# Turning the scaled rows of six chunks by DMA transpose instead of TensorE

## The chip, the cores and the metric

The kernel runs on one core of one Trainium2 chip. The metric is the device time of one execution in microseconds (us). A profiled execution gives a span, from the first to the last instruction, and a time of its own that is a little longer.

## The reference

Polynomial-sketch attention for 4 batches x 4 heads x 1088 positions with head size 32, followed by a two-layer network with squared ReLU over all 4352 tokens:

```python
def phi(x):
    a = np.einsum('rd,bhsd->bhsr', S1, x)          # r = 8
    b = np.einsum('rd,bhsd->bhsr', S2, x)
    return np.einsum('bhsi,bhsj->bhsij', a, b).reshape(*x.shape[:-1], 64)

q_p, k_p = (phi(q), phi(k))
kv = np.einsum('bhsf,bhsd->bhfd', k_p, v)
z = np.sum(k_p, axis=2)
num = np.einsum('bhsf,bhfd->bhsd', q_p, kv)
den = np.einsum('bhsf,bhf->bhs', q_p, z)[..., None] + 1e-06
attn = num / den
x = attn.transpose(0, 2, 1, 3).reshape(4352, 128)  # heads side by side
h = np.maximum(x @ w_in, 0.0)                      # w_in 128 x 2048
out = h * h @ w_out                                # w_out 2048 x 128
```

## The kernel before

The tokens of a batch are cut into two chunks of 512 (`(b, g)` with `b` 0 to 3 and `g` 0 or 1) and 64 leftover rows. Chunk (0,0) is done in two halves of 256 at the start, and the leftover rows of all four batches make one chunk of 256 near the end. So there are ten chunks in the order: two halves, (0,1), (1,0), (1,1), (2,0), (2,1), (3,0), the leftover rows, (3,1).

*The network.* `first_product` (L694) makes `pg`, 128 hidden features x 512 tokens, from `xT` (the chunk's rows turned so that the 128 features lie on the partitions) and a block of `w_in`, both in 16 bits; ScalarE takes the ReLU into `gt` (L701), VectorE squares it into `g` (L702, `g2` in the source). `block` multiplies `g` by a block of `w_out` into `po` (L721; L731 for the last chunk). There are 16 such steps to a chunk. `first_product` runs up to two steps ahead of `block`, over the border to the next chunk if that one is in the list `chunks`. The results are scaled back by `beta` and stored by `store` (L667, L675).

*The attention.* It is cut into generators whose pieces are worked in between the steps of the network: `add_work` puts them in lanes, and after each step `pump(2)` lets up to two lanes advance. `yield n` in a generator asks for n steps until its next piece; `drain` runs all lanes to their end. `k_gen` makes the sums over keys (`kvbd`) of the next batch, `q_gen` the features of the queries of a chunk, and `x_gen` the numerators `nd`, the scaled rows `xs` and `xT`.

*The turning of xs.* `normalize` computes for each row the denominators, a scale per row and `beta`, and writes `xs` (VectorE, L469: 128 positions x 512, four blocks of 128 features, 16 bits). Two steps later TensorE transposes the four blocks into a PSUM tile `x_ps` (L484), and ScalarE copies it to `xT` (L487). Then `chunk_of` puts the chunk in `chunks`.

*The loads.* All loads and stores are issued on SP. The `k`, `v` and `q` of batch b+2 are loaded in the middle of the work on batch b, after the first `drain`; they are pinned: `keep_in_program_order` holds them in the place that the source gives them. `v` is brought by 32 small DMAs (L110, tile `v_turned`), which GpSimd copies into `v_main` (L359). The chunks that are not in `BY_PE` have their q, and for b > 1 their k, turned in 32 x 32 blocks by VectorE (`turned`, L241, tile `xt`).

The start, up to `by_hand.close()`, is in an order written by hand; after it a scheduler orders the instructions of each engine by its own estimates. Each engine works its queue in order.

Of the kernel before, what the change touches and what calls it, by code (L numbers as in the profile page):

```python
# [12 lines left out]
def _v(t: bass.AP, off: int, free, p0: int = 0, n: int = 128):  # L13

    p = list(t.ap)[0]
    return bass.AP(
        t.tensor, t.offset + p0 * p[0] + off, [[p[0], n]] + [list(d) for d in free]
    )
# [3 lines left out]
def kernel(  # L22
# [11 lines left out]
    nc = tc.nc  # L34
# [374 lines left out]
    def numerators(b, phT, m, T=4, tag="nd", bufs=1):  # L409
        nd = pspool.tile([128, 256 * T], F32, name="nd", tag=tag, bufs=bufs)  # L410
        for t in range(T):
            for pr in range(2):
                tiled(
                    nd, 256 * t + 2 * VW * pr, 2 * VW, phT[pr], 128 * t,
                    kvbd[b % 2][:, 2 * VW * pr : 2 * VW * pr + 2 * VW],
                    m=m,
                )
        return nd
# [4 lines left out]
        nc.gpsimd.memset(t[:], 1.0)  # L423
    made_norms = [0]

    def normalize(nd, T, xT, col):


        small = [apool.tile([128, 16], F32, name=f"small{i}", tag=f"small{i}") for i in range(4)]
        den, rden, top, rs = small  # L430
        rtop = rtops[made_norms[0] % len(rtops)]
        made_norms[0] += 1
        mm = apool.tile([128, 4], F32, tag="mm")
        mp = apool.tile([128, 4], F32, tag="mp")
        rm = apool.tile([128, 4], F32, tag="rm")
        beta = apool.tile([128, 4], F32, tag="beta", bufs=4)
        xs = apool.tile([128, 512], F16, tag="xs")
        num = _v(nd, 0, [[256, T], [VW, 4], [1, 32]])
        nc.vector.tensor_scalar(
            out=den[:, 0 : 4 * T], in0=_v(nd, D, [[256, T], [VW, 4]]),  # L440
            scalar1=1e-6, scalar2=None, op0=add,
        )
        nc.vector.reciprocal(rden[:, 0 : 4 * T], den[:, 0 : 4 * T])
        nc.vector.tensor_reduce(
            out=_v(top, 0, [[4, T], [1, 4]]), in_=num,
            axis=AX, op=amax, apply_absolute_value=True,
        )
        yield 1
        nc.vector.tensor_tensor(  # L449
            out=_v(rtop, 0, [[5, T], [1, 4]]),  # L450
            in0=_v(top, 0, [[4, T], [1, 4]]),
            in1=_v(rden, 0, [[4, T], [1, 4]]),
            op=mult,
        )
        nc.vector.tensor_reduce(  # L455
            out=mm[:, 0:T], in_=_v(rtop, 0, [[5, T], [1, 5]]),
            axis=AX, op=amax, apply_absolute_value=True,
        )
        nc.vector.reciprocal(rm[:, 0:T], mm[:, 0:T])
        nc.vector.scalar_tensor_tensor(  # L460
            out=_v(rs, 0, [[4, T], [1, 4]]),
            in0=_v(rden, 0, [[4, T], [1, 4]]),
            scalar=1024.0,
            in1=_v(rm, 0, [[1, T], [0, 4]]),
            op0=mult,
            op1=mult,
        )
        yield 1
        nc.vector.tensor_tensor(  # L469
            out=_v(xs, 0, [[128, T], [32, 4], [1, 32]]),  # L470
            in0=num,
            in1=_v(rs, 0, [[4, T], [1, 4], [0, 32]]),
            op=mult,
        )
        nc.gpsimd.tensor_scalar(  # L475
            out=mp[:, 0:T], in0=mm[:, 0:T], scalar1=1.0 / 1024.0, scalar2=None, op0=mult
        )
        nc.gpsimd.tensor_tensor(
            out=beta[:, 0:T], in0=mp[:, 0:T], in1=mp[:, 0:T], op=mult
        )  # L480
        yield 2
        x_ps = pspool.tile([128, 512], F16, tag="ms", bufs=2)
        for t in range(T):
            nc.tensor.transpose(  # L484
                x_ps[:, 128 * t : 128 * t + 128], xs[:, 128 * t : 128 * t + 128], iden16[:, :]
            )
        nc.scalar.copy(xT[:, col : col + 128 * T], x_ps[:, 0 : 128 * T])  # L487
        return beta
# [5 lines left out]
    def chunk_of(b, g, xT, beta):  # L494
        at = out.offset + (b * S + 4 * g) * E
        if (b, g) in BY_PE:
            dsts = [(bass.AP(out.tensor, at, [[NJ * E, 128], [1, 512]]), 0, 128, 0, 512)]
        else:
            dsts = [
                (  # L500
                    bass.AP(
                        out.tensor, at + j * E, [[NJ * E, 32], [32 * NJ * E, 4], [1, E]]
                    ),
                    32 * j, 32, 0, 512,
                )
                for j in range(4)
            ]
        chunks.append((xT, 4, [(beta, 4)], dsts))

    def half_gen(phT, t0, m, tag, bufs):  # L510

        nd = numerators(0, phT, m, 2, tag, bufs)
        yield 1
        xT = apool.tile([128, 256], F16, name="xT_h", tag=f"xT_h{t0}", bufs=1)
        beta = yield from normalize(nd, 2, xT, 0)
        dst = bass.AP(out.tensor, out.offset + t0 * E, [[NJ * E, 128], [1, 256]])
        chunks.append((xT, 2, [(beta, 2)], [(dst, 0, 128, 0, 256)]))
        yield 1

    def x_gen(b, g, phT, m=32):  # L520
        nd = numerators(b, phT, m)
        yield 1
        xT = apool.tile([128, 512], F16, name="xT", tag="xT", bufs=3)
        beta = yield from normalize(nd, 4, xT, 0)
        chunk_of(b, g, xT, beta)
        yield 1

    def q_gen(b, g, outer, m=32):
        eng = nc.scalar
        if (b, g) == (0, 1):  # L530
            ph = features(ab_second[0], 4, "ph_q", eng, outer)
        else:
            xt = proj_t(q_sb[b], g, 4, eng) if (b, g) in BY_PE else turned(q_sb[b], g)
            yield 1
            ph = proj(xt, 4, "ph_q", eng, outer, m=m)
        yield 3
        phT = []
        for pr in range(2):
            phT.append(feature_t(ph, 4, pr, eng))
            yield 1  # L540
        yield from x_gen(b, g, phT)
# [19 lines left out]
    def qrem_num_gen(b):  # L561
        r, u = b // 2, b % 2
        if u == 0:
            nd_rem[r] = cpool.tile([128, 4 * VW], F32, name=f"nd_rem{r}")
        nd = pspool.tile([128, 512], F32, name="nd", tag="ms", bufs=2)
        for pr in range(2):
            tiled(
                nd, 2 * VW * pr, 2 * VW, phT_rem[r][pr], 64 * u,
                kvbd[u][:, 2 * VW * pr : 2 * VW * pr + 2 * VW], 64, 64 * u,
            )  # L570
        nc.vector.tensor_copy(
            out=_v(nd_rem[r], 0, [[1, 4 * VW]], 64 * u, 64),
            in_=_v(nd, 0, [[1, 4 * VW]], 64 * u, 64),
        )
        yield 1
        if u == 1:
            beta = yield from normalize(nd_rem[r], 1, xT_rem, 128 * r)
            rem_beta.append((beta, 1))
            for w in range(2):
                dst = bass.AP(  # L580
                    out.tensor, out.offset + ((2 * r + w) * S + SM) * E, [[E, 64], [1, E]]
                )
                rem_dst.append((dst, 64 * w, 64, 128 * r, 128))
            if r == 1:
                chunks.append((xT_rem, 2, rem_beta, rem_dst))
# [292 lines left out]
```

## Time and profile before

| | |
|---|---|
| median of 3 runs | 212.81 us (212.15 to 213.9) |
| profiled execution, its own time | 213.51 us |
| its span | 211.4 us |
| granted TensorE clock | 0.999 |
| TensorE busy | 202.8 us, 96% |
| VectorE busy | 146.2 us, 69% |
| ScalarE busy | 111.8 us, 53% |
| GpSimd busy | 48.0 us, 23% |
| transposes of xs (L484) | 34, six groups of four in the chunks that are changed |
| copies to xT (L487), 128x512 | 7, 585 ns each |

Busy time is the sum over an engine's instructions; a group's row has the line, the engine, the operation, what it writes and reads, its shape and number, then busy time, the mean ns of one, and the idle time of the engine before them with what ended it. `PE` is TensorE, `PEld` its weight loads, `DVE` VectorE, `ACT` ScalarE, `POOL` GpSimd, and `SPq` SP issuing a DMA. A row of the timeline has start and duration in us, the engine, the line and the instruction; in brackets is how long the engine sat idle before it, and what released it.

### The profile page before, as it was taken

Reading aid. Unit: us, or ns where it says so; the run is one execution under the profiler, and the core shown is the slowest. Engines: PE = TensorE matmul, PEld = TensorE weight load, DVE = VectorE, ACT = ScalarE, POOL = GpSimd, SP = SyncE. Lnnn points to the kernel's source line nnn. Section 1 sums busy time; section 2 is a strip of 40 time slices with the busy share of each in tenths; the row PEclk is TensorE's granted clock in tenths of the full one; section 3 lists DMA queues with packets and bytes.
Section 4 is the critical chain, followed back from the end, with each engine's and each line's share of the span. In section 5 each row is a group of like instructions: output and inputs, shape, how many; then the busy total and the mean of one; then the engine's idle time right before and its main releaser. Section 6 shows DMA issues by size and latency. Waiting matters only on the chain.

```text
span 211.4 us, 5448 instructions
## 1 busy us (share of the span) xinstructions
PE 202.8 (96%) x2241; PEld 127.4 (60%) x2241; DVE 146.2 (69%) x281; ACT 111.8 (53%) x212; POOL 48.0 (23%) x66
## 2 busy tenths in 40 slices
PE   6988999999999999999999999999999899999993
PEld 5876878764644545545545555455445454789992
DVE  3559766936586899867777677567858777766662
ACT  2448664354556455455465553655465456555550
POOL 1003364104040683004130971022102210000000
PEclk9999999999999999999999999999999999999999
DMA  6999101422400421131000200001000100010001
GB/s 167 243 355 291 18 0 31 129 36 31 137 0 0 142 46 31 31 109 50 3 2 2 54 3 3 0 15 38 0 0 4 48 3 0 2 50 16 12 0 50
DMA packets 25736, 11.36 MB, mean 54 GB/s; under 512 B 13296, under 2 KB 25328, under 8 KB 25712
## 3 DMA queue, kind: packets, MB, share of 16 engines
q1 hardware_dynamic: 25632, 11.02, 19.9%
q8 instruction: 17, 0.28, 0.5%
q14 instruction: 7, 0.06, 0.1%
q10 hardware_dynamic: 80, 0.01, 0.0%
HBM read 8.79 MB, written 2.23 MB: 52 GB/s over the span
## 4 chain that ended last, share of the span: by engine, by line
PE 89%; DVE 6%; DMA 1%; ACT 1%; issue 1%; ACTq 0%; DVEq 0%
PE po L721 47%; PE pg L694 14%; PE po L731 7%; PE ab_ps L204 5%; PE nd L204 4%; PE kv_ps L309 3%; PE t_ps L386 3%; DVE g L702 3%; PE xt_ps L224 2%; PE o_ps L638 2%; DMA s_nat<-in_S_dram 1%; PE x_ps L484 1%; ACT gt L701 1%; DVE xs L469 1%; DVE rtop L449 1%
## 5 line engine op out<-in xcount | busy, mean ns | idle before, releaser
L702 DVE TENSOR_TENSOR g<-gt 128x512 f32<-128x512 f32 x136 | 102.3, 763 | 44.1 <-ACT gt L701 42.0
L721 PE MATMUL po<-g,w_o 128*128 128x512 f32 (+1 forms) x288 | 123.5, 525 | 1.2 <-DVE g L702 1.2
L701 ACT ACTIVATE gt<-pg 128x512 f32<-128x512 f32 x136 | 81.3, 599 | 47.7 <-PE pg L694 46.1
L721 PEld LDWEIGHTS po<-g,w_o 128*128 128x128 f32 x288 | 52.3, 191 | 26.5 <-issue 8.4
L245 POOL TENSOR_TENSOR ph<-ab 128x512 f32<-128x512 f32 (+1 forms) x27 | 32.6, 1234 | 61.5 <-ACT ab L59 61.5
L694 PE MATMUL pg<-xT,w_in 128*128 128x512 f16 x112 | 42.5, 381 | 0.0
L694 PEld LDWEIGHTS <-w_in 128*128 128x128 f16 x160 | 15.5, 99 | 20.1 <-issue 16.4
L475 POOL TENSOR_SCALAR mp<-mm 128x4 f32<-128x4 f32 (+2 forms) x11 | 5.4, 494 | 61.6 <-DVE mm L455 61.6
L731 PEld LDWEIGHTS po<-w_o,g 128*128 128x128 f32 x128 | 16.6, 192 | 0.6
L731 PE MATMUL po<-w_o,g 128*128 128x128 f32 x128 | 16.6, 275 | 0.0
L59 ACT COPY sb<-t_ps 128x512 f32<-128x512 f32 (+1 forms) x18 | 9.1, 515 | 9.9 <-PE t_ps L386 9.8
L204 PEld LDWEIGHTS ab_ps<-w_bd,xt 128*32 128x32 f32 (+1 forms) x476 | 9.6, 119 | 6.4 <-issue 3.5
L59 ACT COPY ab<-ab_ps 128x256 f32<-128x256 f32 (+1 forms) x19 | 6.3, 338 | 13.1 <-PE ab_ps L204 11.5
L204 PE MATMUL ab_ps<-w_bd,xt 128*32 128x64 f32 (+1 forms) x476 | 12.9, 230 | 0.0
L386 PEld LDWEIGHTS t_ps<-iden,ph 128*128 128x128 f32 x60 | 7.5, 141 | 6.8 <-issue 4.9
L204 PEld LDWEIGHTS nd<-kvbd,sb 128*32 128x32 f32 x480 | 8.0, 109 | 6.0 <-issue 3.6
L204 PE MATMUL nd<-kvbd,sb 128*32 128x66 f32 x480 | 9.9, 222 | 0.6 <-issue 0.6
L386 PE MATMUL t_ps<-iden,ph 128*128 128x128 f32 x60 | 9.2, 273 | 0.0
L487 ACT COPY xT<-x_ps 128x512 f16<-128x512 f16 x7 | 4.1, 585 | 9.6 <-PE x_ps L484 9.6
L59 ACT COPY xt<-xt_ps 128x512 f32<-128x512 f32 (+1 forms) x11 | 5.2, 471 | 6.4 <-PE xt_ps L224 6.3
L667 DVE TENSOR_TENSOR o_sb<-o_ps,beta 128x512 f32<-128x512 f32 (+2 forms) x10 | 5.5, 557 | 3.1 <-PE o_ps L638 2.9
L694 PE MATMUL pg<-xT_h,w_in 128*128 128x256 f16 x32 | 6.0, 273 | 0.6 <-ACT gt L701 0.5
(70 smaller groups left out, 120.9 us busy)
## 6 DMA issues: line engine op xcount, KB each, us to landing
t<-in_k_dram SPq DMA_DIRECT2D x3, 512.0 KB, 4.0
t<-in_q_dram SPq DMA_DIRECT2D x3, 512.0 KB, 4.0
out_dram<-o_sb SPq DMA_DIRECT2D x20, 64.0 KB, 1.8
w_in<-in_moe_w_in_dram SPq DMA_DIRECT2D x2, 512.0 KB, 5.0
w_o<-in_moe_w_out_dram SPq DMA_DIRECT2D x2, 512.0 KB, 7.5
v_turned<-in_v_dram SPq DMA_DIRECT2D x64, 16.0 KB, 1.7
k_sb<-in_k_dram SPq DMA_DIRECT2D x2, 256.0 KB, 3.3
q_sb<-in_q_dram SPq DMA_DIRECT2D x2, 256.0 KB, 4.9
```

What stands on the lines that cost most here:

```text
L59: return nc.scalar.copy(dst, src)
L204: nc.tensor.matmul(out_ps[p0 + c : p0 + c + m, c0 : c0 + w], lhsT[:, l0 + c : l0 + c + m], rhs,)
L245: eng.tensor_tensor(out=_v(ph, 256 * t0, [[64, 4 * w], [8, 8], [1, 8]]), in0=_v(ab, 64 * t0, [[16, 4 * w], [1, 8], [0, 8]]), in1=_v(ab, 64 ...
L309: nc.tensor.matmul(self.ps[c : c + self.m, at : at + w], _v(ph, c0 + 128 * pr + c, [[1, self.m]], p0, n), v_of(2 * pr + c // 64), start=c ...
L386: nc.tensor.transpose(t_ps[:, 128 * t : 128 * t + 128], ph[:, 256 * t + 128 * pr : 256 * t + 128 * pr + 128], iden[:, :],)
L475: nc.gpsimd.tensor_scalar(out=mp[:, 0:T], in0=mm[:, 0:T], scalar1=1.0 / 1024.0, scalar2=None, op0=mult)
L667: nc.vector.tensor_tensor(out=_v(o_sb, 128 * t0, [[128, n], [1, 128]]), in0=_v(po, 128 * t0, [[128, n], [1, 128]]), in1=_v(beta, 0, [[1, n ...
L694: nc.tensor.matmul(pg[:, nt * i : nt * i + nt], w_in[:, 128 * (c + i) : 128 * (c + i) + 128], xT[:, 0:nt],)
L701: last_relu[0] = nc.scalar.activation(gt[:, :], pg[:, :], Relu).ins
L702: nc.vector.tensor_tensor(out=g2[:, :], in0=gt[:, :], in1=gt[:, :], op=mult)
L721: last_product[0] = nc.tensor.matmul(po[0][:, 0:nt], w_o[:, 128 * c : 128 * c + 128], g2[:, nt * i : nt * i + nt], start=(c == 0), stop=(c ...
L731: nc.tensor.matmul(po[t // 2][:, 128 * (t % 2) : 128 * (t % 2) + 128], g2[:, 128 * t : 128 * t + 128], w_o[:, 128 * c : 128 * c + 128], st ...
```

## The change

The four transposes on TensorE and the copy on ScalarE are replaced by one DMA transpose, issued on SP, that reads `xs` and writes `xT`, both in SBUF. It is done for the six chunks (1,0) to (3,1); chunk (0,1), the two halves and the leftover rows keep the old way. The chunk is put in the list four steps later than the DMA is issued, for chunk (0,1) four steps later than its copy. All lines behind the change move by up to six: `pg` becomes L700, its ReLU L707, the square L708, `po` L727 and L737, the store L681, and the DMA transpose is L482.

```diff
-    def normalize(nd, T, xT, col):
+    def normalize(nd, T, xT, col, by_dma=False):
...
         nc.gpsimd.tensor_tensor(
             out=beta[:, 0:T], in0=mp[:, 0:T], in1=mp[:, 0:T], op=mult
         )
+        if by_dma:
+            nc.sync.dma_start_transpose(
+                _v(xT, col, [[128, T], [1, 128]]), xs[:, 0 : 128 * T]
+            )
+            return beta
         yield 2
         x_ps = pspool.tile([128, 512], F16, tag="ms", bufs=2)
...
-        beta = yield from normalize(nd, 4, xT, 0)
+        beta = yield from normalize(nd, 4, xT, 0, by_dma=(b, g) != (0, 1))
+        yield 4
         chunk_of(b, g, xT, beta)
```

## The prediction

> **What bounds the kernel now.** I read first the page's shares by engine and the chain that ended last, then the timeline of TensorE around one of the six removed groups, then the two queues that the change moves work onto (SP) or past (VectorE).
>
> ```profile
> span 211.4 us, 5448 instructions
> PE 202.8 (96%) x2241; PEld 127.4 (60%) x2241; DVE 146.2 (69%) x281; ACT 111.8 (53%) x212; POOL 48.0 (23%) x66
> PE 89%; DVE 6%; DMA 1%; ACT 1%; issue 1%; ACTq 0%; DVEq 0%
> L484 PE MATMUL x_ps<-iden,xs 128*128 128x128 f16 x34 | 3.7, 220 | 0.2 <-DVE xs L469 0.2
> L487 ACT COPY xT<-x_ps 128x512 f16<-128x512 f16 x7 | 4.1, 585 | 9.6 <-PE x_ps L484 9.6
> ```
>
> TensorE is busy 96% of the span and is 89% of the chain. Whatever leaves its queue is a gain; whatever it has to wait for is a loss. ScalarE, at 53%, is not the bound, so evictions taken from it bring nothing by themselves. The x_ps group holds 34 transposes: 24 belong to the six chunks of the change, the other ten to the two halves, chunk (0,1) and the leftover rows. What one group of four costs TensorE is read from the distance between neighbouring `pg` products:
>
> ```profile
> 61.22 0.38 PE L694 MATMUL pg<-xT,w_in 128*128 128x512 f16 x1
> 61.44 1.12 PE L721 MATMUL po<-g,w_o 128*128 128x512 f32 x2
> 62.40 0.39 PE L484 MATMUL x_ps<-iden,xs 128*128 128x128 f16 x4
> 62.62 0.38 PE L694 MATMUL pg<-xT,w_in 128*128 128x512 f16 x1
> 63.70 0.38 PE L694 MATMUL pg<-xT,w_in 128*128 128x512 f16 x1
> 64.77 0.38 PE L694 MATMUL pg<-xT,w_in 128*128 128x512 f16 x1
> ```
>
> With the four transposes in between, the step is 62.62 - 61.22 = 1.40 us; without, 1.07 or 1.08. One group costs 0.33 us. The product at 64.77 is the first that reads the new chunk's xT.
>
> **Part 1, the gain.** Six groups x 0.33 = 1.9 us leave TensorE's path. Six evictions x 0.585 = 3.5 us leave ScalarE; they lie beside products (the step after one, 62.62 to 63.70, is the usual 1.08), so I count 0 for them. In the built program the order of TensorE's queue is otherwise that of before, so the late addition of the chunk (the new `yield 4`) moves no product. Gain: 1.9 us, and no more than that.
>
> **Part 2, the latency L of the transposing DMA.** It may start when xs is written and must have landed before the chunk's first `pg`. The room is that product's start, less 0.33 (its queue is now shorter), less 0.1 (its weight load, which carries the wait), less the end of xs. For (1,0), xs ends at 60.06 + 0.69 = 60.75: 64.77 - 0.43 - 60.75 = 3.6 us. The same reading gives 3.6 for (2,0) (xs ends 106.71, product 110.72), 3.6 for (3,0) (152.17, 156.16), 5.6 for (2,1) (129.40, 135.46) and 12.7 for (3,1) (174.89, 187.98). What covers the transfer is four steps of 1.07 us; anything over the room stops TensorE one for one, since its queue is in order.
>
> No transpose by DMA is in this trace, so L is bounded by rows:
>
> ```profile
> q1 hardware_dynamic: 25632, 11.02, 19.9%
> out_dram<-o_last SPq DMA_DIRECT2D x2, 128.0 KB, 1.9
> v_turned<-in_v_dram SPq DMA_DIRECT2D x64, 16.0 KB, 1.7
> v_rem<-in_v_dram SPq DMA_DIRECT2D x4, 32.0 KB, 4.1
> ```
>
> From below: a plain 128 KB transfer, which is what xs holds, lands in 1.9 us. From above: a packet of the queue took 19.9% x 16 x 211.4 / 25632 = 26 ns of one engine. The built instruction gives its unit as 16 rows by 128 columns, so a unit has 16 elements for each of 128 partitions; written as separate pieces that is 4,096 of them, 4,096 x 26 ns / 16 = 6.7 us, and with the 1.7 of a small DMA 8.4. I take 4.1, the row of short pieces, near the geometric middle. Then (1,0), (2,0) and (3,0) stick out by 0.5 us each, 1.5 together; (2,1) and (3,1) are covered.
>
> The skill's pages disagree. The Trainium skill, "Advanced Engine Details and Errata", section X-Bar Transpose (TRN2), holds such transfers as fast as regular ones; L would then be near the plain row, this term 0, and the sum below -0.1 us, 212.7. "VectorE: DVE Perf Modes", section The three transpose paths, speaks against the change: 1309 ns by DMA against 390 on TensorE for one 128x128 block. Four in a row are an estimate of 5.2 us, this term 4.8, and the sum +6.1 us, 218.9. The trace's 0.33 us for four blocks already beats the page's TensorE price.
>
> **Part 3, what waits behind the transpose on SP.** SP's queue is in order. In the built program the transpose of (1,1) stands ahead of the pinned loads for batch 3 (k, 32 pieces of v, q), which before went out as soon as the store ahead of them had. Before, and the same load for batch 2, for which VectorE did wait:
>
> ```profile
> 35.82 0.38 SPq L79 DMA_DIRECT2D t<-in_k_dram  x1
> 39.89 0.71 DVE L241 STREAM_TRANSPOSE xt<-t 128x512 f32<-128x512 f32 x1 [0.23 <-DMA t<-in_k_dram]
> ...
> 70.93 0.39 SPq L79 DMA_DIRECT2D t<-in_k_dram  x1
> 71.37 18.85 SPq L110 DMA_DIRECT2D v_turned<-in_v_dram  x32
> 90.26 0.43 SPq L79 DMA_DIRECT2D t<-in_q_dram  x1
> ...
> 84.56 0.71 DVE L241 STREAM_TRANSPOSE xt<-t 128x512 f32<-128x512 f32 x1
> 85.19 0.65 DVE L469 TENSOR_TENSOR xs<-nd,small 128x512 f16<-128x512 f32 x1
> 87.16 0.71 DVE L241 STREAM_TRANSPOSE xt<-t 128x512 f32<-128x512 f32 x1
> ```
>
> The k load of batch 3 goes out at 70.93, 13.6 us before its first reader at 84.56. Now it stands behind a wait for xs of (1,1). In the built program the two turns of that k (84.56 and 87.16) come later on VectorE, behind the copies of kvbd, so xs ends 0.54 us earlier against its neighbours, and 0.33 for the group saved in (1,0): 85.84 - 0.87 = 84.97. The transpose goes out at 85.05, the k load 0.45 later (four stores took 1.78 to issue) at 85.50. With the 4.07 us of batch 2 (35.82 to 39.89) it lands at 89.57; that is the lower end. The upper: it runs in the same queue q1 behind the transpose and lands no sooner than 85.05 + 4.1 + 2.27, where 2.27 is 4.07 less the 1.8 of a small store: 91.42. Rows for either are lacking; I take the middle, 90.5.
>
> VectorE is at the first turn at about 87.9 and stops there, 2.6 us, with the squares g queued behind it. The order is turn, g, turn, g: the first g is done 0.71 + 0.69 = 1.40 after the landing, the second 2.80. Their readers, the `po` pairs at 90.22 and 91.30 of before, are now due 0.66 earlier, 89.56 and 90.64. TensorE stops for the later of landing + 1.40 - 89.56 and landing + 2.80 - 90.64, which is landing - 87.8. That is 90.5 - 87.8 = 2.7 us (1.8 at the lower end, 3.6 at the upper). The xT of (1,1) has 90.00 - 0.43 - 85.30 = 4.3 us of room and lies within this wait. The v pieces (18.85 us) and q follow until about 105; the copies of v on GpSimd (106.18) and the turn of that q (118.31) still find them, and with four stores (1.8 us) SP is free near 107, when xs of (2,0), pushed back by the stall, is just ready. I count 0 there; without the stall it would be about 1 us.
>
> **Sum.** -1.9 + 1.5 + 2.7 = +2.3 us. The profiled run took 213.51 us, span 211.4 and 2.1 around it; it becomes 215.8. The median of the three runs is 212.81, 0.7 less: 215.1, or 1.1% slower. About 1% is what a measurement of this kernel can tell from no change (the three runs lie within 0.8%).
>
> **Rivals.**
> *The transfer is hidden and the late k costs little (not slower).* One mechanism: L at or under 3.6 us, so every room covers it, and k at its lower end. -1.9 + 1.8 = -0.1: 212.7. Were k's wait absent as well, -1.9: 210.9. For it: DMA engines that are idle then (slices 12 and 13 of the span, at (1,0), and 21, at (2,0), show 0 tenths) and the 1.9 us row. Against: batch 2, where VectorE waited for k although no transpose was ahead. It decides from L = 3.6.
> *The transfer becomes the bound.* At L = 7, three chunks lose 3.4 each, (2,1) 1.4, and k, between 89.57 and 94.32, 4.1: 10.2 + 1.4 + 4.1 - 1.9 = +13.8, 226.6. At 8.4 it is +20, 233. For it: 26 ns a packet. Against: 4,096 separate pieces are only inferred from the unit's shape.
> *It does not use a fast path and moves element by element.* 65,536 elements x 26 ns / 16 = 106 us for each of six: beyond 700 us. Against: the instruction is one of its own kind, not a strided copy.
>
> **How the numbers follow.** Forecast (L 3.6 to 5.5): 0.45; hidden: 0.30; bound: 0.22; elementwise: 0.03. The likeliest gives 215.1, its own range 212.7 to 220. For 8 in 10 I leave out the upper half of the bound case, the elementwise one, and the best corner of the hidden one: 211.2 to 226. Faster by over 1% needs more than the 1.9 us there is: 0.05 for what I do not see. Within 1%: the hidden case less that, and a fifth of the forecast: 0.34. Slower: 0.61.
>
> **What would show it.** Right: no x_ps groups at six places; distances of 1.07 there; VectorE's L241 waiting 2 to 4 us for `t<-in_k_dram` near 88 us; weight loads of L700 (the line of `pg` after the change) waiting about half a microsecond for xT at (1,0), (2,0), (3,0). Wrong: a transpose issue that lands within 3.6 us or takes over 5.5; SP issuing k of batch 3 near 71 us as before; a L241 that does not wait.

## The result, and the profile after

The changed kernel takes 215.35 us (median of 22 runs, 214.03 to 217.82), the kernel before 212.83 (22 runs). The ratio is 1.0112, 95% interval 1.0093 to 1.0132: about 2.4 us slower, 2.0 to 2.8. Of the 22 runs eight show a granted TensorE clock of 1.0 and have a median of 214.77 us, the others 0.984 or 0.992 and a median of 216.0 us. The profiled execution, one of the eight, took 214.32 us, with a span of 212.6. That span is only 1.2 us above the one of before. But the first product starts at 17.72 us before and at 16.48 after, a difference of 1.24 us that arises in a stretch where no instruction was changed, so the spans are compared here step by step and not as totals.

The page of the changed kernel, in its parts: span, busy time, the large queue, the chain by engine, the group of VectorE's block turns, and the new DMA with its time from issue to landing.

```profile
span 212.6 us, 5409 instructions
PE 201.0 (95%) x2217; PEld 124.7 (59%) x2217; DVE 145.3 (68%) x281; ACT 108.9 (51%) x206; POOL 47.8 (22%) x66
q1 hardware_dynamic: 28896, 11.81, 21.1%
PE 82%; DVE 8%; DMA 3%; ACT 2%; issue 2%; ACTq 0%; SPq 0%; DVEq 0%
L241 DVE STREAM_TRANSPOSE xt<-t 128x512 f32<-128x512 f32 x9 | 6.2, 701 | 3.5 <-DMA t<-in_k_dram 3.5
xT<-xs SPq DMA_TRANSPOSE x6, 2.3
```

The group of the block turns before:

```profile
L241 DVE STREAM_TRANSPOSE xt<-t 128x512 f32<-128x512 f32 x9 | 6.2, 700 | 0.2 <-DMA t<-in_k_dram 0.2
```

TensorE has 24 matmuls fewer and is busy 1.8 us less, yet its share of the chain fell from 89% to 82%: VectorE and DMA came in. The group rows point at the reason: before the block turns of L241, VectorE now sits idle 3.5 us for the k load, where it was 0.2. The DMA transposes themselves land in 2.3 us (the median of the six), and the queue q1 moved 28896 - 25632 = 3264 packets more, 544 for each of six.

The timeline at (1,0) shows the gain and the room:

```profile
60.08 1.30 SPq L482 DMA_TRANSPOSE xT<-xs  x1
60.52 0.38 PE L700 MATMUL pg<-xT,w_in 128*128 128x512 f16 x1
60.74 1.12 PE L727 MATMUL po<-g,w_o 128*128 128x512 f32 x2
61.70 0.38 PE L700 MATMUL pg<-xT,w_in 128*128 128x512 f16 x1
62.77 0.38 PE L700 MATMUL pg<-xT,w_in 128*128 128x512 f16 x1
63.85 0.38 PE L700 MATMUL pg<-xT,w_in 128*128 128x512 f16 x1
```

The step that held the group, 1.40 us before, is now 61.70 - 60.52 = 1.18. It did not fall to 1.07, so the group cost 0.22 and not 0.33. The product at 63.85 is the first that reads the new xT, and it comes on the beat of 1.08: 60.08 + 2.3 = 62.4 is early enough.

The timeline at (1,1) shows the loss. First the products of before, then the changed kernel:

```profile
90.00 0.38 PE L694 MATMUL pg<-xT,w_in 128*128 128x512 f16 x1
91.08 0.38 PE L694 MATMUL pg<-xT,w_in 128*128 128x512 f16 x1
92.15 0.38 PE L694 MATMUL pg<-xT,w_in 128*128 128x512 f16 x1
```

```profile
83.76 0.69 DVE L469 TENSOR_TENSOR xs<-nd,small 128x512 f16<-128x512 f32 x1
84.48 1.20 SPq L482 DMA_TRANSPOSE xT<-xs  x1
85.77 0.54 SPq L79 DMA_DIRECT2D t<-in_k_dram  x1
88.89 0.38 PE L700 MATMUL pg<-xT,w_in 128*128 128x512 f16 x1
90.58 0.71 DVE L241 STREAM_TRANSPOSE xt<-t 128x512 f32<-128x512 f32 x1 [3.30 <-DMA t<-in_k_dram]
91.21 0.65 DVE L708 TENSOR_TENSOR g<-gt 128x512 f32<-128x512 f32 x1
91.92 1.12 PE L727 MATMUL po<-g,w_o 128*128 128x512 f32 x2 [2.65 <-DVE g L708]
92.88 0.38 PE L700 MATMUL pg<-xT,w_in 128*128 128x512 f16 x1
94.07 0.38 PE L700 MATMUL pg<-xT,w_in 128*128 128x512 f16 x1
```

Read the second view from the top. SP waits for xs, spends 1.20 us on issuing the transpose, and only then sends the k load of batch 3, at 85.77 instead of 70.93. VectorE waits 3.30 us for its landing, the square of L708 stands behind it, and the `po` pair behind the square. The two products at 88.89 and 92.88 are 3.99 apart, the next two 1.19; before, the same steps were 91.08 - 90.00 = 1.08 and 1.07. That is 2.91 + 0.12 = 3.03 us.

Set against each other product by product, the two profiles differ in these steps: six groups, -1.30 us together (0.20 to 0.22 each, at (1,1) net of sums over keys that became 0.14 slower); the wait for k, +3.03; and the sums over keys near 131 us, +0.13. The sum is +1.86. One more step of +0.53 lies near 42 us, ahead of anything that was changed for TensorE:

```profile
42.56 0.42 PE L204 MATMUL nd<-kvbd,sb 128*32 128x66 f32 x7 [0.56 <-issue]
41.85 0.42 PE L204 MATMUL nd<-kvbd,sb 128*32 128x66 f32 x7 [1.09 <-issue]
```

The first row is of before, the second of the changed kernel; `issue` is idle time in which the engine waited for nothing that the profile shows. This step is taken up below.

### The profile page after: what moved, and what is told of

Same layout as the page of the kernel before. It is cut to its first block, busy times and chain, and to the rows that moved or that the text cites. A ratio compares the mean times of both kernels' runs of the same rounds, so it can differ in the third digit from the quotient of the medians.

```text
span 212.6 us, 5409 instructions
## 1 busy us (share of the span) xinstructions
PE 201.0 (95%) x2217; PEld 124.7 (59%) x2217; DVE 145.3 (68%) x281; ACT 108.9 (51%) x206; POOL 47.8 (22%) x66
## 3 DMA queue, kind: packets, MB, share of 16 engines
q1 hardware_dynamic: 28896, 11.81, 21.1%
## 4 chain that ended last, share of the span: by engine, by line
PE 82%; DVE 8%; DMA 3%; ACT 2%; issue 2%; ACTq 0%; SPq 0%; DVEq 0%
PE po L727 44%; PE pg L700 13%; PE po L737 7%; PE nd L204 4%; PE ab_ps L204 4%; DVE g L708 4%; PE t_ps L386 3%; PE kv_ps L309 3%; DMA t<-in_k_dram 2%; PE xt_ps L224 2%; PE o_ps L644 2%; ACT gt L707 1%; DMA s_nat<-in_S_dram 1%; DVE xs L469 1%; DVE xt L241 1%
## 5 line engine op out<-in xcount | busy, mean ns | idle before, releaser
L708 DVE TENSOR_TENSOR g<-gt 128x512 f32<-128x512 f32 x136 | 101.6, 758 | 42.4 <-ACT gt L707 40.7
L727 PE MATMUL po<-g,w_o 128*128 128x512 f32 (+1 forms) x288 | 123.7, 526 | 3.9 <-DVE g L708 3.9
L707 ACT ACTIVATE gt<-pg 128x512 f32<-128x512 f32 x136 | 81.2, 599 | 57.2 <-PE pg L700 55.6
L727 PEld LDWEIGHTS po<-g,w_o 128*128 128x128 f32 x288 | 52.1, 191 | 31.4 <-issue 10.8
L700 PE MATMUL pg<-xT,w_in 128*128 128x512 f16 x112 | 42.5, 381 | 0.0
L700 PEld LDWEIGHTS <-w_in 128*128 128x128 f16 x160 | 15.5, 99 | 21.4 <-issue 17.6
L737 PEld LDWEIGHTS po<-w_o,g 128*128 128x128 f32 x128 | 16.6, 191 | 0.6
L737 PE MATMUL po<-w_o,g 128*128 128x128 f32 x128 | 16.6, 275 | 0.0
L204 PEld LDWEIGHTS ab_ps<-w_bd,xt 128*32 128x32 f32 (+1 forms) x476 | 8.9, 113 | 6.7 <-issue 3.5
L204 PE MATMUL ab_ps<-w_bd,xt 128*32 128x64 f32 (+1 forms) x476 | 12.2, 224 | 0.2
L241 DVE STREAM_TRANSPOSE xt<-t 128x512 f32<-128x512 f32 x9 | 6.2, 701 | 3.5 <-DMA t<-in_k_dram 3.5
L700 PE MATMUL pg<-xT_h,w_in 128*128 128x256 f16 x32 | 6.0, 274 | 0.6 <-ACT gt L707 0.5
```

Source lines behind the costliest of these rows:

```text
L204: nc.tensor.matmul(out_ps[p0 + c : p0 + c + m, c0 : c0 + w], lhsT[:, l0 + c : l0 + c + m], rhs,)
L241: nc.vector.transpose(out=xt[:, :], in_=_v(src, 128 * g, [[NJ * D, 4], [1, 128]]))
L700: nc.tensor.matmul(pg[:, nt * i : nt * i + nt], w_in[:, 128 * (c + i) : 128 * (c + i) + 128], xT[:, 0:nt],)
L707: last_relu[0] = nc.scalar.activation(gt[:, :], pg[:, :], Relu).ins
L708: nc.vector.tensor_tensor(out=g2[:, :], in0=gt[:, :], in1=gt[:, :], op=mult)
L727: last_product[0] = nc.tensor.matmul(po[0][:, 0:nt], w_o[:, 128 * c : 128 * c + 128], g2[:, nt * i : nt * i + nt], start=(c == 0), stop=(c ...
```

## The experiments

Theory A: the loss is the k load of batch 3 behind the transpose of (1,1) on SP; the transposes themselves are hidden. Theory B: each DMA transpose costs about the same, 0.4 us, by its transfer or by what it disturbs.

**Five chunks by DMA, all but (1,1).**

```diff
-        beta = yield from normalize(nd, 4, xT, 0, by_dma=(b, g) != (0, 1))
-        yield 4
+        by_dma = (b, g) not in ((0, 1), (1, 1))
+        beta = yield from normalize(nd, 4, xT, 0, by_dma=by_dma)
+        if by_dma:
+            yield 4
```

> Five chunks by DMA; (1,1) is turned on TensorE as before, so the loads of batch 3 go out near 71 us again. Theory A (the loss is the k load of batch 3 behind the transpose of (1,1)): five groups x 0.21 us saved, about 0.1 lost at the sums over keys near 131 us, no wait of VectorE for k: 0.9 us under the kernel before, ratio 0.996. Theory B (each transpose by DMA costs about the same, 2.4 us / 6): +2.0 us, ratio 1.009. In the trace by A: the L241 of k at 84 to 87 us without a wait, the matrix products of the sums over keys near 86 us at 1.30 us and near 131 us at 1.43.

Measured: ratio 0.9933, interval 0.9905 to 0.9961, 1.4 us faster than the kernel before. Theory B is out: five sixths of the transposes bring a gain. The timeline of this kernel has the second k turn without a wait, and the two sums over keys, the first with no transpose in flight, the second with that of (2,1):

```profile
85.57 0.70 DVE L241 STREAM_TRANSPOSE xt<-t 128x512 f32<-128x512 f32 x1
84.40 1.29 PE L309 MATMUL kv_ps<-v_main,ph 128*32 128x33 f32 x128
128.26 1.42 PE L309 MATMUL kv_ps<-v_main,ph 128*32 128x33 f32 x128
```

**Only (1,1) by DMA.** The same edit with `by_dma = (b, g) == (1, 1)`.

> Only (1,1) by DMA, the other five on TensorE as before. Theory A: the whole wait is kept, +3.0, less one group of 0.21: +2.8 us over the kernel before, ratio 1.013, slower than with all six. Theory B: +0.4 us, ratio 1.002. In the trace by A: one L241 that waits some 3.3 us for the k load.

Measured: 1.0166 (1.0126 to 1.0206), 3.5 us slower. One transpose of six brings more than the whole loss, which is what A says; the size is above the 2.8 expected, at the edge of the interval (2.7 to 4.4). Its timeline:

```profile
85.84 1.31 SPq L482 DMA_TRANSPOSE xT<-xs  x1
87.25 0.52 SPq L79 DMA_DIRECT2D t<-in_k_dram  x1
91.86 0.71 DVE L241 STREAM_TRANSPOSE xt<-t 128x512 f32<-128x512 f32 x1 [3.16 <-DMA t<-in_k_dram]
86.31 1.50 PE L309 MATMUL kv_ps<-v_main,ph 128*32 128x33 f32 x128
133.27 1.30 PE L309 MATMUL kv_ps<-v_main,ph 128*32 128x33 f32 x128
```

**All six by DMA, the k load of batch 3 alone moved ahead.** This keeps everything of the change but one place in SP's order.

```diff
-            k_sb[b + 2] = load(k, b + 2, "k_sb", True)
+            if b == 0:
+                k_sb[b + 2] = load(k, b + 2, "k_sb", True)
...
     for b in range(B):
+        if b == 1:
+            k_sb[3] = load(k, 3, "k_sb", True)
```

> All six by DMA; the k load of batch 3 alone stands ahead of the transpose of (1,1), the 32 pieces of v and the q stay behind it. Theory A with k alone to blame: six groups x 0.21 saved, 0.2 lost at two sums over keys: 1.0 us under the kernel before, ratio 0.995. If v, q or the stores behind them cost as well (the transpose of (2,0) comes behind them on SP): 0 to +1 us, ratio 1.000 to 1.005, with weight loads of L700 waiting at (2,0). Theory B: +2.4, ratio 1.011.

Measured: 0.996 (0.9931 to 0.9989), 0.85 us faster than before. Moving one load turned 2.4 us of loss into a gain. The second guess came true as well, on a small scale. With v and q still behind the transpose of (1,1), SP issues (2,0) late:

```profile
104.17 1.91 SPq L681 DMA_DIRECT2D out_dram<-o_sb  x4
104.69 0.69 DVE L469 TENSOR_TENSOR xs<-nd,small 128x512 f16<-128x512 f32 x1
106.19 1.20 SPq L482 DMA_TRANSPOSE xT<-xs  x1
109.50 0.10 PEld L700 LDWEIGHTS <-w_in 128*128 128x128 f16 x1 [0.99 <-DMA xT<-xs]
109.51 0.39 PE L700 MATMUL pg<-xT,w_in 128*128 128x512 f16 x1 [0.17 <-DMA xT<-xs]
```

xs is ready at 105.38 and goes out 0.8 us later, when the four stores are issued; with their data under way it lands after 3.3 us instead of 2.3, and the first product is late by 0.32 (109.51 - 108.11 is 1.40, the beat 1.08). Without the long stall in front of it, the place on SP that the changed kernel did not feel costs something here.

**All six by DMA, k, v and q of batch 3 all ahead.**

```diff
+    def load_batch(b):
+        k_sb[b] = load(k, b, "k_sb", True)
+        v_sb[b] = load_v(b)
+        q_sb[b] = load(q, b, "q_sb", True)
...
     for b in range(B):
+        if b == 1:
+            load_batch(3)
...
         if b + 2 < B:
-            k_sb[b + 2] = load(k, b + 2, "k_sb", True)
-            v_sb[b + 2] = load_v(b + 2)
-            q_sb[b + 2] = load(q, b + 2, "q_sb", True)
             if b == 0:
+                load_batch(b + 2)
```

> All six by DMA; k, v and q of batch 3 all stand ahead of the transpose of (1,1). Theory A: 1.0 us under the kernel before, ratio 0.995, and the L241 of k without a wait. Theory B: +2.4, ratio 1.011. A later store of chunk (0,1) behind the pieces of v costs nothing, as its buffer is written again only 25 us later.

Measured: 0.9948 (0.9918 to 0.9978), 1.1 us faster than before, as expected. The later store cost nothing that can be seen.

**All six by DMA, issued on ScalarE's queue.** `nc.sync.dma_start_transpose` becomes `nc.scalar.dma_start_transpose`.

> All six by DMA, but issued on ScalarE's queue; SP has the loads of batch 3 near 71 us again. Theory A: no wait for k, six groups x 0.21 saved, 0.2 lost at two sums over keys, but ScalarE is held 1.2 us at each issue and the ReLU behind it comes late; the squares have about 0.4 us to spare, so up to 0.8 us lost at each of six: -1.0 + 0 to 4.8 us, ratio 0.995 to 1.018, and in the trace each loss stands behind a DMA issue of ScalarE. Theory B (the transfer itself costs): +2.4 whatever the queue, ratio 1.011, with VectorE's first L241 of k not waiting.

Measured: 0.994 (0.9912 to 0.9967), 1.3 us faster, just under the lower end of 0.995. That each issue would hold up the ReLU was right, that TensorE would feel it was not:

```profile
59.73 1.28 ACTq L482 DMA_TRANSPOSE xT<-xs  x1
60.16 0.38 PE L700 MATMUL pg<-xT,w_in 128*128 128x512 f16 x1
61.05 1.30 ACT L707 ACTIVATE gt<-pg 128x512 f32<-128x512 f32 x2 [0.96 <-PE pg L700]
61.34 0.38 PE L700 MATMUL pg<-xT,w_in 128*128 128x512 f16 x1
62.41 0.38 PE L700 MATMUL pg<-xT,w_in 128*128 128x512 f16 x1
```

ScalarE is held from 59.73 to 61.01, two ReLUs run back to back behind it, and the products still come 1.18 and 1.07 apart, the distances of the changed kernel. The two steps of prefetch absorb it.

**All seven on SP, with the loads of batches 2 and 3 ahead.** `by_dma=True`, and `load_batch(b + 2)` at the head of the work on batches 0 and 1.

> Chunk (0,1) by DMA as well, with the loads of batches 2 and 3 both ahead of the transposes. Theory A: like the version with the loads of batch 3 first, less one more group of 0.22 and one eviction that the first product waits for, and more traffic early: -1.0 to -1.8 us against the kernel before, ratio 0.992 to 0.995. If the early loads of batch 2 hold up the loads of the start: 0 to +2 us, ratio 1.000 to 1.009, with the loss before 40 us.

Measured: 1.0137 (1.0089 to 1.0186), 2.9 us slower: neither guess. In the profile the first product starts at 17.43 us, against 17.72 before, so nothing shows that the loads of the start were held up; the loss is at (0,1):

```profile
38.07 0.69 DVE L469 TENSOR_TENSOR xs<-nd,small 128x512 f16<-128x512 f32 x1
41.17 1.80 SPq L94 DMA_DIRECT2D t<-in_q_dram  x2
43.07 1.30 SPq L482 DMA_TRANSPOSE xT<-xs  x1
47.42 0.11 PEld L700 LDWEIGHTS <-w_in 128*128 128x128 f16 x2 [2.13 <-DMA xT<-xs]
38.82 1.63 PE L309 MATMUL kv_ps<-v_main,ph 128*32 128x33 f32 x128
```

xs is ready at 38.76, but six small loads of the leftover rows (the last two in the second line) stand ahead on SP; the transpose goes out 4.3 us late and, with their data under way, takes 4.35 to land. The first product of (0,1) loses 2.7 us against the kernel before, of which some 0.3 is the stretch near 42 us. It is the order on SP again, the other way round: at (1,1) a load stood behind a transpose, here a transpose stands behind loads. With the gains of the later groups the steps come to +1.4 at the last product; the rest of the 2.9 us is not in this profile.

**All seven on ScalarE's queue,** which tests that reading. `by_dma=True` in the kernel with ScalarE's queue. Against the version with all seven on SP two things differ: the queue of the transposes, and the loads, which stand where they stood before the change.

> Chunk (0,1) as well, all seven DMA transposes issued on ScalarE's queue, the loads where they were before the change. Theory A (what cost time with all seven on SP was again a place behind other transfers on SP): the DMA of (0,1) goes out when xs is ready near 39 us, its first product comes near 45 us, so nothing waits: as with six on ScalarE's queue, and 0.2 to 0.9 less for the group and the copy of (0,1): -1.0 to -2.0 us against the kernel before, ratio 0.991 to 0.995. Theory C (chunk (0,1) has too little room for a DMA wherever it is issued, or turning the transposed key tiles by VectorE in the new order costs): +1 to +2.5, ratio 1.005 to 1.012, with weight loads of L700 waiting for xT near 45 us.

Measured: 0.9931 (0.9899 to 0.9964), 1.5 us faster than the kernel before. The DMA of (0,1) goes out when xs is ready, and its first product waits for nothing:

```profile
38.56 1.28 ACTq L482 DMA_TRANSPOSE xT<-xs  x1
44.79 0.59 PE L700 MATMUL pg<-xT,w_in 128*128 128x512 f16 x2
```

Chunk (0,1) had room enough; what stood ahead on SP's queue was the trouble. Against six on ScalarE's queue the further gain, 0.2 us, is within the intervals. Five of the seven versions beat the kernel before and the changed one; their intervals overlap, so none is named best.

## Why the prediction was right, and where its steps were not

Forecast +2.3 us, measured +2.4. The place and the mechanism of the loss are shown by the experiments. The agreement of the total is in good part luck. One of the three terms was absent (1.5 forecast, 0 found), the gain was 0.6 smaller and the wait 0.3 larger; with the sums over keys, which had no term, the steps make +1.9, and the rest of the measured 2.4 is in no term of the prediction. One of its own signs of being wrong came as well: the transpose lands within 3.6 us, and no weight load of L700 waits for xT in the changed kernel.

*The gain: 1.9 forecast, 1.30 found.* The step of 1.40 was put down to the group entirely. It also held a wait for VectorE's square, which a row that was shown told: the `po` pair at 61.44 took 1.12 and not 1.02. The same 1.12 stands at 60.74 after the change, without a group. A distance between two neighbours is the cost of what stands between them only if everything else in it has its usual length.

*The latency: 4.1 forecast, 2.3 found; the term 1.5, found 0.* Issuing takes 1.20 of the 2.3. The upper bound failed in its count of pieces: 544 packets to a transpose, which for 128 KB is about 240 bytes each, and not 4,096. The nearest row was the plain 128 KB transfer with its 1.9, and not the row of short pieces. The statement of the Trainium skill, "Advanced Engine Details and Errata", section X-Bar Transpose (TRN2), that such transfers are as fast as regular ones, agrees roughly with this case as to the landing, 2.3 us against the plain 1.9; the issue, 1.20 against some 0.4, it does not tell. The estimate from the Trainium skill, "VectorE: DVE Perf Modes", section The three transpose paths, four blocks in a row at 5.2 us, does not agree: one instruction brings all four in 2.3. The page's own 1309 ns, for a single block, no run here measures.

*The wait for k: 2.7 forecast, 3.03 found.* The chain of steps held to the end: late issue, VectorE's wait (2.6 forecast, 3.30 found), a square late, a `po` pair late. Two terms were low. Issuing the transpose was priced like a store, 0.45 us, and the k load went out 1.29 after it (84.48 to 85.77); and the k load took 90.58 - 85.77 = 4.81 us from issue to VectorE's start, against 4.07 with nothing ahead. Together that is 1.58 above the lower end, of which the middle of the bounds covered 0.93. The second square, on the other side, was done 2.48 us after the landing and not 2.80. That the first turn starts at 90.58, beside the forecast 90.5, is chance: the changed kernel's profile runs 0.9 us ahead of the other there (83.79 for the product at 84.71).

*The place of (2,0) on SP: 0 forecast behind the stall, about 1 us without it.* 0 found, and 0.32 without the stall: there the transpose landed 0.8 + 3.3 = 4.1 us after xs, and the room that the prediction read at (2,0) is 3.6.

*The rivals.* "The transfer is hidden" was right on the transfer, which never stopped TensorE in the changed kernel (its condition, at most 3.6 us, held with 2.3), and wrong on the late k at its lower end, 1.8 against 3.03. "The transfer becomes the bound" and the elementwise one are refuted by the 2.3 us.

*What stays open.* The steps in the profiles sum to +1.86 us and the medians differ by 2.5. Most of this gap goes with the granted clock: the profile had 1.0, and the eight runs with 1.0 have a median 1.9 us above the 212.83 of the kernel before, of which 53 of the 59 runs made beside the experiments show 0.995 or more. Clocks under 0.995 are frequent in the three versions that lose 2.7 us or more at one place (14 of 22 runs of the changed kernel, 2 of 6 with only (1,1), 5 of 6 with all seven on SP) and rare in the other five (at most one run of each). Whether the loss of TensorE's time brings them about was not tried. With only (1,1) by DMA a gap shows too: steps of +2.8, measured +3.5.

The stretch near 42 us accounts for +0.53 in the profile of the changed kernel; in others whose order of instructions on TensorE is the same there it is between 0 (five by DMA) and 0.36 (only (1,1)). It is time in which TensorE waits for nothing that the profile shows, and one profile of each kernel does not tell whether the change has a part in it.

## What to carry to other kernels

A DMA that waits for a result of the kernel holds everything issued behind it on the same queue until that result is there; before putting one on a queue that also carries prefetches, list what the source order puts behind it, and what those feed. Here the transposes were well hidden and worth about 1 us (0.85 to 1.5 in five versions), and one load behind one of them cost 3. The repair is an order, either the loads ahead of the transpose or the transposes on a queue without loads, and after each repair the next transfer that stands ahead has to be looked for.

## What the runs showed of the hardware that was not expected

A DMA transpose of 128 x 512 elements of 16 bits holds the issuing queue 1.19 to 1.31 us on SP and 1.21 to 1.29 on ScalarE, against 0.38 to 0.54 for the plain loads of 512 KB in the rows shown here (the q load of batch 3 in the changed kernel, not shown, took 1.37). It lands 2.3 us after the start of its issue (median of six), 3.3 behind four stores and 4.35 behind six small loads.

The sums over keys, 128 small matmuls, took 1.29 or 1.30 us with no transpose in flight and 1.42 to 1.50 with one, and moved with it: in the kernel with all but (1,1) only the one near 128 us is slow, in the kernel with only (1,1) just the one near 86. The amount of DMA traffic alone does not order these times: beside plain pieces at 76 to 79 GB/s, near 38 us in the kernel before and the changed one, the sums took 1.30; with a transpose in flight they took 1.42 at 56 GB/s and 1.43 at 92 GB/s; and in the version with all seven on SP they took 1.63 beside loads and stores at 197 GB/s, without a transpose. What slows them was not tried by itself.
